# Moving the stores, the loads and the order of the units in an attention + gated-MLP kernel

## The chip, the cores and the metric

The kernel runs on one core of one Trainium2 chip. The time is device time in microseconds (us) of one execution. Executions of the same kernel spread by 1 to 3% within one call here, so every comparison of a few us is made with several runs, and the ratios quoted are the mean time of one kernel's fast runs over that of the other's of the same rounds; they are not quite the ratio of the medians that stand beside them. A run counts as slow when it is over 1.5% above the fastest run of the same kernel, or one die's clock is low; only fast runs enter a ratio.

Engines: PE is TensorE (matmuls), PEld its weight loads, DVE is VectorE, ACT is ScalarE, POOL is GpSimd, SP is SyncE, which here only issues DMAs. In these traces an instruction that waits holds what stands behind it in its engine's queue; the store on ACT below, behind which ACT stood idle for 2.30 us ahead of its next exponential, is an example.

## The reference, cut to what matters

```python
# q, k, v: [8 batches, 8 heads, 576, 64], float32
scores = q @ k.T / 8;  mask: 0 <= i - j < 64         # a sliding window of 64 keys
x = softmax(scores) @ v                               # -> [8, 576, 512]
h = relu(x @ w_in);  u, v = h[..., :512], h[..., 512:]
v_n = layer_norm(v)                                   # over the 512
v_s = w_spatial @ v_n + b_spatial                     # over the 576 positions
out = (u * v_s) @ w_out                               # float32
```

## The kernel before

For each batch, two chains of units run interleaved: the MLP of batch *a* and the attention of batch *a+1*. A string gives the order in which the units are put into the engines' queues; there is no other schedule.

| unit | PE does | ACT, DVE, POOL do |
|---|---|---|
| T*s* (batches 0 to 3) | transposes k and q of head pair *s* | copies of the result ("tr", turned k and q) |
| R*s* or T*s* (batches 4 to 7) | nothing | DVE turns k and q in 32 by 32 blocks |
| A*s* | scores of pair *s* ("sc"), product of pair *s−1* ("oz") | ACT exp, DVE mask; ACT ln, exp(−) ("ln", "zi"), DVE multiply to give "x" |
| F | – | the pending normalisation (zi, x), at once |
| V*j* | `x @ w_in[:, 512:]` for 128 positions ("pv") | ACT relu ("vs"), DVE statistics ("st", "mv") |
| Q | V of the last 64 positions, and the last 64 outputs of batch *a−1* | the same, and a store |
| L | – | layer norm: ACT ln, exp; DVE five "vn" |
| U*m*, G*m*, O*j* | `w_in[:, :512]` ("pu"), spatial ("ps"), `w_out` ("po") | ACT relu; DVE u·v_s ("g"); ACT copy to "ob", store |

"p0003" is V of batch 0 for the first 128 positions, summed over head pairs 0 to 2 (from 0 up to, not including, 3); "p0034" adds pair 3 and "o0" is the relu and the statistics that follow; W is the transposition of the spatial weights. Casts of k, q and v to 16 bits ("nk", "nq", "vn") and the shifted copy of v ("vs<-vn") run on POOL. "X4 of batch b" below means the last x (the remainder of 64 positions) of batch b.

The parts that the change touches:

```python
def load_pairs(b):                     # batches 0 to 3
    ...
    for s in range(4):
        for x in "kq": load_four(b, x, s)
        load_v_pair(b, s, nc.sync)
        if s == 2:
            for x in "kq": load_rest(b, x)     # the last 64 positions of k and q
    load_v_rem(b, nc.sync)

def T_out(b, s):                       # PSUM -> SBUF, y = 0 for k, 1 for q
    ...   (act_copy if b == 0 and y == 1 else dve_copy)(o[:, y, s, 0:512], tp[y][:, :])

def store(b, j, ob, p0):
    (nc.scalar if b < 3 else nc.sync).dma_start(out[b, ...], ob[...])
# ob = mpool.tile([128, 512], f32, tag="ob", bufs=3, ...)

for a in range(1, B):
    if a == 1: batch_in(2)                         # POOL casts of batch 2
    if a + 2 < B: load (a + 2)                     # at the start of the stage
    if a + 2 < B and a > 1: batch_in(a + 2)
    if a == 1:   run(a, "p0034 o0 p0134 o1 p0234 o2 p0334 o3 Q L U0 T0 U1 T1 A0 U2 ..."); batch_in(3)
    elif a == 2: run(a, "V0 T0 V1 T1 A0 V2 V3 Q T2 A1 L U0 U1 U2 T3 A2 ...")
    elif a == 3: run(a, "V0 V1 V2 V3 Q L T0 U0 U1 T1 A0 U2 ...")
    else:        run(a, "V0 V1 A0 V2 V3 Q A1 L U0 U1 U2 A2 U3 U4 G0 A3 ... R0 O0 O1 A5 O2 R1 O3")
```

The softmax here doesn't subtract the row's maximum and nothing guards it: scores larger than these inputs give would overflow.

## Time and profile before

260.36 us, median of three runs (258.87 to 261.31). I read the profile by stages. A stage goes from X4 of one batch to X4 of the next; it holds the MLP of that batch and the attention of the next. The table of windows of the kernel before, cut at those moments (columns: stretch in us, its length, busy time of each engine with the number of its instructions, the granted TensorE clock as a share of full speed, the busy share of the DMA engines, GB/s):

```profile
core 0: us, PE busy (x) PEld busy (x) DVE busy (x) ACT busy (x) POOL busy (x), PEclk, DMA share, GB/s
0.00:72.05 72.05, 56.59 (x575) 30.98 (x576) 40.80 (x90) 32.22 (x53) 47.80 (x81) 0.86 1.09 241
72.05:105.54 33.49, 27.02 (x314) 15.57 (x313) 21.48 (x41) 18.22 (x32) 20.73 (x30) 0.95 0.68 126
105.54:132.59 27.05, 26.05 (x315) 14.72 (x314) 20.04 (x40) 18.23 (x33) 6.90 (x9) 1.00 0.59 139
132.59:164.00 31.41, 25.91 (x357) 13.69 (x355) 21.56 (x38) 18.99 (x36) 13.39 (x14) 0.89 0.34 86
164.00:189.44 25.44, 23.50 (x352) 12.65 (x351) 17.50 (x33) 17.59 (x34) 12.97 (x14) 0.93 0.88 177
189.44:215.76 26.32, 24.37 (x356) 12.84 (x355) 18.30 (x36) 18.19 (x35) 13.02 (x15) 0.94 0.89 181
215.76:239.66 23.90, 22.78 (x356) 12.22 (x355) 16.11 (x33) 18.19 (x35) 0.17 (x1) 1.00 0.15 52
239.66:260.80 21.14, 17.30 (x114) 7.91 (x112) 9.03 (x21) 9.42 (x19) 0.00 (x0) 0.98 0.26 88
```

The first row is the start-up with batch 0 and the attention of batch 1; then one row for each of the batches 1 to 7. The stage without any loads or casts, 215.76 to 239.66, is the measure of the rest: 23.90 us, of which PE works 22.78. The stages of batch 1 (33.49) and of batch 3 (31.41) have little more busy time of PE (27.02 and 25.91) and take much more time; the start-up row holds more work, but PE is idle in 15.5 of its 72.05 us.

The granted clock over the whole span, in 40 slices of 6.5 us, in tenths (page of the kernel before):

```profile
PEclk9996897997598999999997799988999799999999
```

Each digit below 9 is a slice in which PE ran at half clock for a part. Matmuls of 512 columns take 0.63 us there instead of 0.38.

Part of the chain of waits of the kernel before in the hole after batch 0 (start, length, what):

```profile
52.84 6.26 DMA vf<-in_v_dram
...
59.12 0.02 ACTq L478
...
59.17 5.06 DMA out_dram<-ob
...
64.63 0.34 ACTq L478
...
65.01 0.64 ACT zi L423
```

And ACT's own timeline at the same place (start, length, engine, line, operation, in brackets the idle time before it):

```profile
53.45 0.58 ACT L568 COPY ob<-po 128x512 f32<-128x512 f32 x1
55.84 0.39 ACTq L478 DMA_DIRECT2D out_dram<-ob  x1
56.33 1.02 ACT L361 ACTIVATE e<-sc 128x1024 f16<-128x1024 f32 x1 [2.30 <-PE po L565]
```

Waits of PE for x over 162 to 240 us, and for the turned k and q in the stage of batch 3 (us in total, times, longest):

```profile
PE oz L396 <- DVE x L431: 5.0, 3, 2.0
```

```profile
PE sc L319 <- DVE tr L147: 3.8, 1, 3.8
```

The profiled execution took 262.51 us and counts as slow.

### The profile page before, as it was taken

The numbers are of one execution on the slowest core, as the hardware profiler recorded it, in microseconds if no ns is written. First come the engines' busy times: TensorE is split into PE (matmuls) and PEld (weight loads), VectorE is DVE, ScalarE is ACT, GpSimd is POOL, SyncE is SP. The second block draws the span as 40 slices with busy tenths as digits, with TensorE's granted clock in tenths as the row PEclk, the third lists the DMA queues.
The fourth block names the chain that finished last, engine by engine and source line by source line (L and its number), as shares of the span: only waits on it lengthen the run. The fifth ranks groups of instructions, "written<-read, shape, count | busy, mean of one in ns | idle before, by whom it ended". The sixth has DMA issues, their size and how long they took to land.

```text
span 260.8 us, 6702 instructions
## 1 busy us (share of the span) xinstructions
PE 223.5 (86%) x2725; PEld 120.6 (46%) x2725; DVE 164.8 (63%) x326; ACT 151.1 (58%) x271; POOL 115.0 (44%) x161
## 2 busy tenths in 40 slices
PE   8767889983885987999994998979997999899994
PEld 2533336651343653555542554535553555454441
DVE  5465185865268592797657387865796469563840
ACT  1454363255453564587574566875687568957713
POOL 3899258997026559920002980126913591000000
PEclk9996897997598999999997799988999799999999
DMA  6999999999997903877086003899499932004105
GB/s 196 247 250 226 203 244 224 246 241 325 247 180 179 147 3 100 219 149 161 32 239 117 3 3 123 193 201 171 126 227 199 183 114 92 23 4 156 27 0 181
DMA packets 77647, 40.43 MB, mean 155 GB/s; under 512 B 44272, under 2 KB 73008, under 8 KB 77616
## 3 DMA queue, kind: packets, MB, share of 16 engines
q1 hardware_dynamic: 73424, 34.22, 60.1%
q0 software_dynamic: 2224, 2.24, 5.1%
q10 hardware_dynamic: 1968, 3.54, 4.2%
q8 instruction: 21, 0.34, 0.6%
q14 instruction: 10, 0.08, 0.1%
HBM read 32.79 MB, written 9.44 MB: 162 GB/s over the span
## 4 chain that ended last, share of the span: by engine, by line
PE 47%; SPq 17%; DVE 16%; ACT 9%; DMA 7%; issue 3%; ACTq 1%
PE ps L546 11%; PE pv L459 7%; PE po L565 7%; SPq L122 7%; SPq L83 7%; PE pu L526 6%; DMA vf<-in_v_dram 5%; DVE vn L516 5%; DVE st L468 4%; PE oz L396 3%; PE sc L319 3%; SPq L87 3%; DVE x L431 2%; PE oz L406 2%; ACT e L361 2%
## 5 line engine op out<-in xcount | busy, mean ns | idle before, releaser
L361 ACT ACTIVATE e<-sc 128x1024 f16<-128x1024 f32 x32 | 32.8, 1024 | 35.7 <-PE sc L303 21.5
L177 POOL CAST nk<-fk 128x512 f16<-128x512 f32 (+2 forms) x23 | 18.8, 816 | 75.1 <-DVE tr L147 29.2
L431 DVE TENSOR_TENSOR x<-oz,zi 128x512 f16<-128x512 f32 (+1 forms) x40 | 25.3, 634 | 38.6 <-ACT zi L423 38.4
L177 POOL COPY vs<-vn 64x512 f16<-64x512 f16 (+1 forms) x56 | 44.5, 794 | 3.1
L377 DVE TENSOR_TENSOR e<-e,mask 128x1024 f16<-128x1024 f16 x32 | 27.8, 868 | 21.3 <-ACT e L361 21.0
L546 PE MATMUL ps<-wspT,vn 128*128 128x512 f16 (+1 forms) x160 | 39.3, 394 | 0.0
L459 PE MATMUL pv<-win,x 128*128 128x512 f16 (+1 forms) x132 | 34.3, 406 | 0.4 <-ACT vs L466 0.4
L526 PE MATMUL pu<-x,win 128*128 128x512 f16 x128 | 34.3, 418 | 0.0
L565 PE MATMUL po<-wout,g 128*128 128x512 f16 x128 | 31.1, 385 | 0.0
L177 POOL CAST vn<-vf 128x512 f16<-128x512 f32 (+1 forms) x40 | 26.9, 682 | 9.1 <-DMA vf<-in_v_dram 8.3
L468 DVE BATCH_NORM_STATS2 st<-vs 128x6 f32<-128x512 f16 (+1 forms) x40 | 26.9, 673 | 5.3 <-ACT vs L466 4.8
L414 ACT ACTIVATE ln<-oz 128x512 f32<-128x512 f32 (+1 forms) x40 | 22.2, 554 | 12.7 <-PE oz L406 12.3
L466 ACT ACTIVATE vs<-pv 128x512 f16<-128x512 f32 (+1 forms) x40 | 22.7, 596 | 9.0 <-PE pv L459 5.8
L177 POOL CAST nq<-fq 128x512 f16<-128x512 f32 (+2 forms) x27 | 21.3, 790 | 12.8 <-DMA fq<-in_q_dram 10.9
L423 ACT ACTIVATE zi<-ln 128x512 f32<-128x512 f32 (+1 forms) x40 | 23.4, 586 | 4.4 <-ACT ob L568 1.3
L549 DVE TENSOR_TENSOR g<-ps,ru 128x512 f16<-128x512 f32 x32 | 21.8, 686 | 6.6 <-PE ps L546 6.5
L568 ACT COPY ob<-po 128x512 f32<-128x512 f32 x32 | 18.6, 583 | 12.1 <-PE po L565 11.6
L396 PE MATMUL oz<-e,onesK 128*64 128x512 f16 x64 | 13.6, 417 | 13.1 <-DVE x L431 13.1
L546 PEld LDWEIGHTS <-vn 128*128 128x128 f16 (+1 forms) x160 | 15.2, 102 | 16.7 <-issue 1.9
L528 ACT ACTIVATE ru<-pu 128x512 f32<-128x512 f32 x32 | 17.2, 593 | 6.0 <-PE pu L526 6.0
L459 PEld LDWEIGHTS <-x 128*128 128x128 f16 (+1 forms) x132 | 12.8, 104 | 16.1 <-issue 3.2
L526 PEld LDWEIGHTS <-win 128*128 128x128 f16 x128 | 12.2, 105 | 16.0 <-issue 5.5
(97 smaller groups left out, 315.5 us busy)
## 6 DMA issues: line engine op xcount, KB each, us to landing
vf<-in_v_dram SPq DMA_DIRECT2D x40, 128.0 KB, 5.3
out_dram<-ob SPq DMA_DIRECT2D x20, 256.0 KB, 2.0
fk<-in_k_dram SPq DMA_DIRECT2D x32, 144.0 KB, 3.6
fq<-in_q_dram SPq DMA_DIRECT2D x32, 144.0 KB, 4.3
fk<-in_k_dram SPq DMA_DIRECT2D x16, 256.0 KB, 5.2
fq<-in_q_dram SPq DMA_DIRECT2D x16, 256.0 KB, 5.2
vf<-in_v_dram SPq DMA_DIRECT2D x16, 256.0 KB, 5.0
out_dram<-ob ACTq DMA_DIRECT2D x12, 256.0 KB, 3.1
```

The costliest lines, as they stand in the source:

```text
L177: nc.gpsimd.tensor_copy(o, i)
L361: nc.scalar.activation(e2[:, :, :], sc[0][:, :, :], AF.Exp, bias=0.0, scale=0.125)
L377: nc.vector.tensor_tensor(e2[:, :, :], e2[:, :, :], m, ALU.min)
L414: nc.scalar.activation(lnz[:, 0:n], OZ[b, s][:, 1, 0:n], AF.Ln)
L423: nc.scalar.activation(zinv[:, 0:n], lnz[:, 0:n], AF.Exp, bias=0.0, scale=-1.0)
L431: nc.vector.tensor_tensor(x[:, 0:n], oz[:, 0, 0:n], zinv[:, 0:n], ALU.mult)
L459: nc.tensor.matmul(PV[b, j][0:jn, :], xcol(b, r, j), w_in_sb[:, r, 512:1024], start=(r == 0), stop=(r == 3))
L466: nc.scalar.activation(vs[0:jn, :], pv[0:jn, :], AF.Relu)
L468: nc.vector.bn_stats(st6[0:jn, 0:6], vs[0:jn, :])
L526: nc.tensor.matmul(pu[:, :], w_in_sb[:, r, 128 * m:128 * m + 128], X[b, r][:, :], start=(r == 0), stop=(r == 3))
L546: nc.tensor.matmul(ps[:, :], VN[b, kk][0:kn, 128 * m:128 * m + 128], wspT[kk][0:kn, 0:512], start=(kk == 0), stop=(kk == 4))
L565: nc.tensor.matmul(po[:, :], G[b, r][:, 128 * j:128 * j + 128], w_out_sb[:, r, :], start=(r == 0), stop=(r == 3))
```

## The change

In a few words: all stores on the sync queue with five output buffers instead of three; the loads of the next but one batch behind the store in Q; V of batches 0 and 1 summed in two halves, two head pairs each, as the data lands; the turned k and q of the next batch, and the pending normalisation, ahead of layer norm; the copies of turned q on ACT. The diff, cut to its core ("..." and "cut" mark what is left out):

```diff
@@ load_pairs, batch_in: the remainder of k and q after pair 3's k and q, not before
-            load_v_pair(b, s, nc.sync)
-            if s == 2:
+            if s == 3:
                 for x in "kq":
                     load_rest(b, x)
+            load_v_pair(b, s, nc.sync)
@@ T_out: turned q always copied by ACT
-                (act_copy if b == 0 and y == 1 else dve_copy)(o[:, y, s, 0:512], tp[y][:, :])
+                (act_copy if y == 1 else dve_copy)(o[:, y, s, 0:512], tp[y][:, :])
@@ store
-        (nc.scalar if b < 3 else nc.sync).dma_start(out[b, ...], ob[...])
+        nc.sync.dma_start(out[b, ...], ob[...])
-        ob = mpool.tile([128, 512], f32, tag="ob", bufs=3, ...)      # twice
+        ob = mpool.tile([128, 512], f32, tag="ob", bufs=5, ...)
@@ run: loads and casts of batch a+2 in Q, after the store of batch a-1
                 if c == "Q":
                     emit_VO4(a)
+                    if a > 0 and a + 2 < B:
+                        load_any(a + 2)
+                        batch_in(a + 2)
@@ start-up and batch 0 (pairs 0, 1, 2, 3 with the remainder last; more warm-up matmuls; cut)
-    emit_S(0, 4)
-    E_exp(0, 4)
     ...
-    run(0, "p0003 p0103")            # V of batch 0: three of four pairs ...
+    run(0, "p0002 p0102")            # ... or two and two
     emit_P(0, 3)
+    emit_S(0, 4)
+    E_exp(0, 4)
     ...
-    emit_P(0, 4)
-    emit_N1(0, 4)
-    emit_N2(0, 4)
-    run(0, "p0034 o0 p0134 o1 p0234 o2 p0334 o3 Q L U0 U1 U2 U3")
-    run(0, "W0 W1 W2 W3 W4 U4 T0 G0 G1 T1 A0 G2 G3 T2 A1 G4 O0 T3 A2 O1 O2 T4 A3 O3")
-    run(0, "F A4 p1003 p1103 F A5 p1203 p1303 F")
+    emit_P(0, 4)
+    run(0, "p0023 p0123 p0223 p0323 p0034 o0 p0134 o1 p0234 o2 p0334 o3")
+    emit_N1(0, 4)
+    emit_N2(0, 4)
+    run(0, "U0 U1 Q L U2 T0 U3 A0 W0 W1 W2 W3 W4 U4 G0 T1 A1 G1 G2 T2 G3 A2 G4")
+    batch_in(2)
+    run(0, "O0 O1 T3 A3 O2 O3 T4 F A4 F p1002 p1102")
+    run(0, "A5 p1202 p1302 p1023 p1123 p1223 p1323 F")
@@ stages of batches 1 to 7
-  1: "... o3 Q L U0 T0 U1 T1 A0 U2 U3 T2 A1 ... G3 G4 A4 ..."
+  1: "... o3 T0 U0 T1 U1 A0 Q L T2 U2 U3 A1 ... G3 A4 G4 ..."
-  2: "... Q T2 A1 L U0 ..."                +  2: "... Q T2 A1 F L U0 ..."
-  3: "V0 V1 V2 V3 Q L T0 U0 U1 T1 A0 ..."  +  3: "V0 T0 V1 V2 V3 A0 Q F L T1 U0 U1 A1 ..."
-  4 to 7: "... Q A1 L U0 ..."              +  4 to 7: "... Q A1 F L U0 ..."
```

More of the change, by code (lines that the diff above doesn't have):

```diff
@@ L477, in store @@
         jn = 128 if j < 4 else 64
-        (nc.scalar if b < 3 else nc.sync).dma_start(out[b, 128 * j:128 * j + jn, :],
+        nc.sync.dma_start(out[b, 128 * j:128 * j + jn, :],
                                                     ob[p0:p0 + jn, :])
@@ L498, in emit_VO4 @@
             V_out(b, 4)
-        ob = mpool.tile([128, 512], f32, tag="ob", bufs=3, name=f"ob{o}_4")
+        ob = mpool.tile([128, 512], f32, tag="ob", bufs=5, name=f"ob{o}_4")
         nc.scalar.copy(ob[64:128, :], pv[64:128, :])
@@ L566, in emit_O @@
                                  start=(r == 0), stop=(r == 3))
-        ob = mpool.tile([128, 512], f32, tag="ob", bufs=3, name=f"ob{b}_{j}")
+        ob = mpool.tile([128, 512], f32, tag="ob", bufs=5, name=f"ob{b}_{j}")
         nc.scalar.copy(ob[:, :], po[:, :])
@@ L634, in run, with load_any @@
                     state["post"].pop(0)()
+    def load_any(b):
+        if b < NPE:
+            load_pairs(b)
+        else:
+            new_qkv(b)
+            load_batch(b)
     def v_in(b, s):
@@ L647, in batch_in @@
                 pairs_in(b, s, pool_copy, pool_copy)
+                if s == 3:
+                    pairs_in(b, 4, pool_copy, pool_copy)
                 v_in(b, s)
-                if s == 2:
-                    pairs_in(b, 4, pool_copy, pool_copy)
             v_in(b, 4)
@@ L659, in batch_in @@
                 shift_part(b, c // 2, pool_copy)
-    for s in (0, 1, 2, 4, 3):
-        pairs_in(0, s, dve_copy, pool_copy if s != 3 else dve_copy)
-        if s == 4:
-            emit_T(0, 4)
-            continue
+    for s in range(4):
+        pairs_in(0, s, dve_copy, pool_copy if s < 3 else dve_copy)
+        if s == 3:
+            pairs_in(0, 4, pool_copy, pool_copy)
         v_in(0, s)
@@ L670 @@
         T_mm(0, s)
+        if s < 3:
+            warm(2)
         if s > 0:
@@ L677 @@
         E_exp(0, s)
+        if s == 3:
+            T_mm(0, 4)
         if s > 0:
@@ L681 @@
             N_exp(0, s - 1)
-        warm(4)
+        if s < 3:
+            warm(4)
+    T_out(0, 4)
+    E_mask(0, 3)
+    N_mul(0, 2)
     v_in(0, 4)
@@ L687 @@
     batch_in(1)
+    run(0, "p0002 p0102")
+    emit_P(0, 3)
     emit_S(0, 4)
     E_exp(0, 4)
-    E_mask(0, 3)
-    N_mul(0, 2)
-    run(0, "p0003 p0103")
-    emit_P(0, 3)
     emit_N1(0, 3)
@@ L697 @@
     E_mask(0, 4)
-    run(0, "p0203 p0303")
+    run(0, "p0202 p0302")
     emit_P(0, 4)
+    run(0, "p0023 p0123 p0223 p0323 p0034 o0 p0134 o1 p0234 o2 p0334 o3")
     emit_N1(0, 4)
     emit_N2(0, 4)
-    run(0, "p0034 o0 p0134 o1 p0234 o2 p0334 o3 Q L U0 U1 U2 U3")
-    run(0, "W0 W1 W2 W3 W4 U4 T0 G0 G1 T1 A0 G2 G3 T2 A1 G4 O0 T3 A2 O1 O2 T4 A3 O3")
-    run(0, "F A4 p1003 p1103 F A5 p1203 p1303 F")
+    run(0, "U0 U1 Q L U2 T0 U3 A0 W0 W1 W2 W3 W4 U4 G0 T1 A1 G1 G2 T2 G3 A2 G4")
+    batch_in(2)
+    run(0, "O0 O1 T3 A3 O2 O3 T4 F A4 F p1002 p1102")
+    run(0, "A5 p1202 p1302 p1023 p1123 p1223 p1323 F")
     for a in range(1, B):
         if a == 1:
-            batch_in(2)
-        if a + 2 < B:
-            if a + 2 < NPE:
-                load_pairs(a + 2)
-            else:
-                new_qkv(a + 2)
-                load_batch(a + 2)
-        if a + 2 < B and a > 1:
-            batch_in(a + 2)
-        if a == 1:
-            run(a, "p0034 o0 p0134 o1 p0234 o2 p0334 o3 Q L U0 T0 U1 T1 A0 U2 U3 T2 A1 U4 G0 T3 A2 "
-                   "G1 G2 T4 A3 G3 G4 A4 O0 O1 A5 O2 O3")
-            batch_in(3)
+            run(a, "p0034 o0 p0134 o1 p0234 o2 p0334 o3 T0 U0 T1 U1 A0 Q L T2 U2 U3 A1 U4 G0 T3 A2 "
+                   "G1 G2 T4 A3 G3 A4 G4 O0 O1 A5 O2 O3")
         elif a == 2:
-            run(a, "V0 T0 V1 T1 A0 V2 V3 Q T2 A1 L U0 U1 U2 T3 A2 U3 U4 G0 T4 A3 G1 G2 G3 A4 "
+            run(a, "V0 T0 V1 T1 A0 V2 V3 Q T2 A1 F L U0 U1 U2 T3 A2 U3 U4 G0 T4 A3 G1 G2 G3 A4 "
                    "G4 O0 O1 A5 O2 O3")
         elif a == 3:
-            run(a, "V0 V1 V2 V3 Q L T0 U0 U1 T1 A0 U2 U3 A1 U4 G0 G1 A2 G2 G3 A3 G4 O0 A4 R0 O1 O2 "
-                   "A5 R1 O3")
+            run(a, "V0 T0 V1 V2 V3 A0 Q F L T1 U0 U1 A1 U2 U3 U4 A2 G0 G1 A3 G2 G3 A4 G4 R0 O0 O1 "
+                   "A5 O2 R1 O3")
         else:
-            run(a, "V0 V1 A0 V2 V3 Q A1 L U0 U1 U2 A2 U3 U4 G0 A3 G1 G2 G3 A4 G4 R0 O0 O1 A5 O2 R1 O3")
+            run(a, "V0 V1 A0 V2 V3 Q A1 F L U0 U1 U2 A2 U3 U4 G0 A3 G1 G2 G3 A4 G4 R0 O0 O1 A5 O2 R1 O3")
     run(B, "Q")
```

## The prediction

> What bounds the kernel now. One core, eight batches, read as stages (table of windows): start-up 0–33 us; batch 0 with attention of 1, 33–59; a hole 59–67; then 38, 27, 31.6, 26.3, 26.3, 23.8, 21.8 us. The late stages are bound by TensorE: 24.4 of 26.3 us busy at clock 0.94; in the 23.8 us stage (215–239, no loads or casts left) 22.7 at clock 1.00. The others lose time to waits:
> - 59–67: TensorE is busy 3.2 of 8 us, clock 0.68. The chain of waits runs through a store on the ACT queue (5.06 us to landing, behind loads) that holds one of three output buffers; then ACT zi, DVE x, PE oz.
> - 70–84: five layer-norm statistics in series (0.65 + 0.18 us each), five normalisations, 2.73 us together because GpSimd copies meanwhile (0.41 us each undisturbed), and only then the turned k and q (81.0) that the next scores wait for (2.3 us).
> - 137–142: TensorE busy 1.2 of 5 us; the turns of batch 4 stand behind layer norm (wait for DVE tr: 3.8 us).
> - Late: PE oz waits for DVE x, 5.0 us in three waits over 162–240, as x stands behind layer norm; the clock dips after (0.83 in 200–210).
> - Start-up: the remainder of k and q stands before pair 3; batch 0's last projections come after everything.
>
> Each hole also costs clock: the Trainium skill, "TensorE: Matmul & The Clock Gate", section "What's actually happening", says an idle window of about 3.4 us halves the clock. The trace agrees in kind: 512-column matmuls took 0.63 us instead of 0.38 after holes. The slow normalisations match "SBUF — State Buffer", "Who interferes with whom": VectorE and GpSimd exclude one another (1.24 against 0.41 us).
>
> What the change does. Work is the same, but for six warm matmuls (0.26 us each, in waits) and 12 copies of turned q moved from DVE to ACT (0.67 to about 0.6 us). The rest is order:
> - Start-up: pair 3 without the remainder ahead, half of V early: −3.5 us. Weights still bound it: issued at 14.5, 9.8 us to landing.
> - Stores on the sync queue, five buffers, batch 3's loads later: the hole mostly closes, −6 us.
> - Batch 1: turns ahead of layer norm: −6 us.
> - Batch 3: turns spread: −4 us.
> - Normalisation ahead of layer norm: −1 us in each of four stages, clock included.
> - Given back: loads of batches 5 to 7 start at the store in Q, some 6 us later in their stage. Those of k and q took 17 us to the last cast (163.7–180.7), V another 7.5. V would be ready some 7 us into the next stage, where the first attention product wants it at about 6. I add 3 us.
>
> Sum: −20.5. I take 241 us, a little less gain; range 233 to 252. Faster by over 2%: 0.94; within 2%: 0.05; slower: 0.01.
>
> Right if: no output copy on ACT waits for a store; batch 2's first V matmul comes at 88 to 92 us instead of 104; PE waits for DVE tr in batch 3's stage fall below 1 us; PE oz waits for DVE x below 2 us late; the clock holds 1.00 in more slices; TensorE's total busy time falls.
>
> Wrong if: the later loads make VectorE wait for GpSimd's casts in the last turn, or PE for V, in the stages of batches 4 to 6; stores behind loads in the one sync queue still fill five buffers; extra ACT copies delay exp; or the start-up waits for weights, so that reordering it gains nothing.

## The result, and the profile after

The changed kernel took 242.45 us (median of four runs, 241.97 to 245.32) beside 260.84 us for the kernel before (four runs). The ratio of the fast runs is 0.935, with a 95% interval of 0.927 to 0.944. The output is correct. The profiled execution (245.32 us) is the slowest of its four; keep that in mind for single stages.

The same table of windows of the changed kernel, again cut at X4 of each batch:

```profile
0.00:70.01 70.01, 54.04 (x578) 30.14 (x579) 35.98 (x85) 34.66 (x57) 47.95 (x82) 0.88 0.95 200
70.01:96.07 26.06, 24.48 (x309) 14.27 (x308) 17.88 (x37) 20.05 (x36) 11.97 (x19) 1.00 0.68 157
96.07:121.73 25.66, 25.66 (x316) 14.61 (x315) 18.40 (x36) 20.05 (x37) 7.04 (x10) 1.00 0.76 149
121.73:147.11 25.38, 23.19 (x356) 12.69 (x355) 19.54 (x38) 18.45 (x35) 14.75 (x18) 1.00 0.98 203
147.11:170.23 23.12, 22.89 (x356) 12.16 (x355) 17.80 (x35) 18.09 (x35) 10.98 (x12) 1.00 0.95 190
170.23:199.41 29.18, 25.89 (x356) 12.90 (x355) 19.67 (x35) 18.75 (x35) 18.60 (x22) 0.88 0.95 201
199.41:222.53 23.12, 22.76 (x356) 12.21 (x355) 16.11 (x32) 18.17 (x35) 2.85 (x4) 1.00 0.15 53
222.53:243.60 21.07, 17.30 (x114) 7.90 (x112) 9.02 (x20) 9.43 (x19) 0.00 (x0) 0.99 0.26 88
```

| stage | before | after | difference |
|---|---|---|---|
| up to X4 of batch 1 | 72.05 | 70.01 | −2.0 |
| batch 1 | 33.49 | 26.06 | −7.4 |
| batch 2 | 27.05 | 25.66 | −1.4 |
| batch 3 | 31.41 | 25.38 | −6.0 |
| batch 4 | 25.44 | 23.12 | −2.3 |
| batch 5 | 26.32 | 29.18 | **+2.9** |
| batch 6 | 23.90 | 23.12 | −0.8 |
| batch 7 and the end | 21.14 | 21.07 | −0.1 |

Two rows don't fit the total: the start-up gained almost nothing although the hole in it was to close, and the stage of batch 5 lost 6 us against its neighbours (29.18 against 23.12). The granted clock of the changed kernel in 40 slices of 6.1 us:

```profile
PEclk9997599599999999999999999999968999999999
```

Low clock is left in three places: slices 4 and 5, in the start-up, slice 8, in batch 0, and slices 30 and 31, in the stage of batch 5. Read from the records of the clock in the traces, PE had half clock for:

```
before (us):  20.9-27.7  41.4-44.8  61.9-72.1  82.4-85.8  140.4-147.2  174.5-177.9  201.8-205.2   sum 37.6
after  (us):  21.3-31.5  41.8-48.6  178.3-185.1                                                   sum 23.9
```

(the last fall, at the very end, left out). PE's busy time fell from 223.5 to 216.2 us, for the same matmuls and two warm-up matmuls more. Half of the 13.7 us less of half clock is 6.9 us, which is most of it.

Waits of PE of the changed kernel for the turned k and q in the stage of batch 3 (121 to 147 us), and its waits in the late stages (145 to 225 us):

```profile
PE sc L319 <- DVE tr L147: 1.3, 2, 0.9
```

```profile
PE oz L406 <- POOL vs L177: 3.5, 3, 2.1
PE oz L396 <- DVE x L431: 0.4, 1, 0.4
```

The waits for turned k and q and for x, on which the prediction built, are small now. A new one has come: PE waits for POOL's shifted copies of v. And in the start-up (timeline of PE of the changed kernel, and then of the kernel before, at the transposes of the spatial weights, L576):

```profile
22.23 1.89 PE L459 MATMUL pv<-win,x 128*128 128x512 f16 x4 [2.23 <-DMA win<-in_moe_w_in_dram]
...
42.50 0.64 PE L303 MATMUL sc<-tr 64*64 64x128 f16 x16 [3.05 <-DVE tr L180]
43.08 3.64 PE L576 MATMUL wps<-id,wnat 128*128 128x128 f16 x25
```

```profile
38.20 1.98 PE L576 MATMUL wps<-id,wnat 128*128 128x128 f16 x20 [0.58 <-ACT ru L528]
40.74 0.53 PE L576 MATMUL wps<-id,wnat 128*64 128x128 f16 x5 [0.57 <-DVE wspT L180]
```

In the changed kernel PE first stood 2.2 us for the weights `w_in`, then 3.05 us for a turned k that DVE delivers after layer norm, and the transposes behind it took 3.64 us at half clock instead of 2.5.

### The profile page after: what moved, and what is told of

Same layout as the page of the kernel before. It is cut to its first block, busy times and chain, and to the rows that moved or that the text cites. A ratio compares the mean times of both kernels' runs of the same rounds, so it can differ in the third digit from the quotient of the medians.

```text
span 243.6 us, 6712 instructions
## 1 busy us (share of the span) xinstructions
PE 216.2 (89%) x2727; PEld 116.9 (48%) x2727; DVE 154.4 (63%) x313; ACT 157.7 (65%) x283; POOL 114.1 (47%) x162
## 4 chain that ended last, share of the span: by engine, by line
PE 41%; DMA 20%; POOL 11%; ACT 9%; DVE 6%; SPq 6%; issue 5%; POOLq 0%; ACTq 0%
DMA fq<-in_q_dram 15%; PE ps L546 8%; PE pv L459 8%; PE po L565 7%; POOL vs L177 6%; PE pu L526 5%; SPq L117 4%; POOL vn L177 4%; DMA win<-in_moe_w_in_dram 3%; PE oz L396 2%; DMA vf<-in_v_dram 2%; ACT e L361 2%; DVE x L431 2%; PE oz L406 2%; DVE st L468 2%
## 5 line engine op out<-in xcount | busy, mean ns | idle before, releaser
L431 DVE TENSOR_TENSOR x<-oz,zi 128x512 f16<-128x512 f32 (+1 forms) x40 | 25.4, 635 | 29.2 <-ACT zi L423 29.1
L177 POOL CAST nk<-fk 128x512 f16<-128x512 f32 (+2 forms) x24 | 19.8, 825 | 48.2 <-DMA fk<-in_k_dram 39.8
L361 ACT ACTIVATE e<-sc 128x1024 f16<-128x1024 f32 x32 | 32.9, 1027 | 14.4 <-PE sc L303 10.1
L377 DVE TENSOR_TENSOR e<-e,mask 128x1024 f16<-128x1024 f16 x32 | 24.7, 772 | 21.6 <-ACT e L361 21.6
L546 PE MATMUL ps<-wspT,vn 128*128 128x512 f16 (+1 forms) x160 | 38.1, 384 | 0.0
L526 PE MATMUL pu<-x,win 128*128 128x512 f16 x128 | 33.2, 404 | 0.0
L466 ACT ACTIVATE vs<-pv 128x512 f16<-128x512 f32 (+1 forms) x40 | 23.2, 597 | 14.2 <-PE pv L459 12.3
L177 POOL CAST nq<-fq 128x512 f16<-128x512 f32 (+2 forms) x27 | 20.9, 776 | 23.8 <-DMA fq<-in_q_dram 23.7
L177 POOL CAST vn<-vf 128x512 f16<-128x512 f32 (+1 forms) x40 | 25.5, 642 | 12.4 <-DMA vf<-in_v_dram 11.5
L565 PE MATMUL po<-wout,g 128*128 128x512 f16 x128 | 30.1, 379 | 0.0
L423 ACT ACTIVATE zi<-ln 128x512 f32<-128x512 f32 (+1 forms) x40 | 23.7, 593 | 0.9
L546 PEld LDWEIGHTS <-vn 128*128 128x128 f16 (+1 forms) x160 | 14.6, 99 | 15.8 <-issue 0.7
L528 ACT ACTIVATE ru<-pu 128x512 f32<-128x512 f32 x32 | 17.9, 600 | 2.9 <-PE pu L526 2.5
L516 DVE TENSOR_SCALAR vn<-vs,mv,rs 128x512 f16<-128x512 f16 (+1 forms) x40 | 16.6, 482 | 2.4 <-ACT rs L508 2.4
```

Of the source, the lines that this page charges most:

```text
L177: nc.gpsimd.tensor_copy(o, i)
L361: nc.scalar.activation(e2[:, :, :], sc[0][:, :, :], AF.Exp, bias=0.0, scale=0.125)
L377: nc.vector.tensor_tensor(e2[:, :, :], e2[:, :, :], m, ALU.min)
L423: nc.scalar.activation(zinv[:, 0:n], lnz[:, 0:n], AF.Exp, bias=0.0, scale=-1.0)
L431: nc.vector.tensor_tensor(x[:, 0:n], oz[:, 0, 0:n], zinv[:, 0:n], ALU.mult)
L466: nc.scalar.activation(vs[0:jn, :], pv[0:jn, :], AF.Relu)
```

## The experiments

Twelve kernels ran and one more did not build. All twelve gave correct results. "Stage of batch b" is X4 to X4 as above; "X4(1)" is the time at which X4 of batch 1 is done. Medians of different calls come from different chips, so small differences are read from ratios and stages.

| kernel | median, us | ratio to before (fast runs) | X4(1) | stages of batches 1 / 2 / 3 / 4 / 5 / 6 |
|---|---|---|---|---|
| before | 260.36 | 1 | 72.1 | 33.5 / 27.1 / 31.4 / 25.4 / 26.3 / 23.9 |
| changed | 242.45 | 0.935 (0.927 to 0.944) | 70.0 | 26.1 / 25.7 / 25.4 / 23.1 / 29.2 / 23.1 |
| before + stores | 249.54 | 0.967 (0.961 to 0.973) | 64.3 | 32.9 / 26.5 / 30.6 / 23.0 / 24.2 / 23.9 |
| before + five buffers | 262.08 | 1.012 (1.000 to 1.024) | 72.4 | 33.6 / 27.1 / 31.4 / 25.5 / 26.3 / 23.9 |
| before + turns first | 252.33 | 0.980 (0.964 to 0.996) | 71.9 | 30.5 / 27.0 / 25.3 / 24.7 / 26.4 / 23.9 |
| before + norm first | 253.76 | 0.984 (0.974 to 0.994) | 72.6 | 33.9 / 26.7 / 30.3 / 22.3 / 23.1 / 23.1 |
| changed, q copies on DVE | 245.43 | 0.951 (0.945 to 0.956) | 72.6 | 27.1 / 26.1 / 24.7 / 23.9 / 24.3 / 23.9 |
| changed, loads early | 240.61 | 0.929 (0.922 to 0.936) | 69.7 | 26.1 / 25.7 / 25.2 / 23.1 / 23.1 / 23.1 |
| changed, old start-up | 238.31 | none (three of four runs slow) | 65.8 | 26.0 / 25.8 / 26.7 / 23.1 / 28.6 / 23.1 |
| changed, remainder first | 242.16 | 0.932 (0.919 to 0.945) | 69.1 | 26.4 / 25.7 / 24.8 / 23.7 / 24.7 / 23.5 |
| changed, W ahead of A0 | 239.39 | 0.926 (0.915 to 0.937) | 64.6 | 26.1 / 25.7 / 26.5 / 23.1 / 26.5 / 23.1 |
| changed, both mended, loads early | 236.21 | 0.905 (0.889 to 0.920) | 67.8 | 26.4 / 25.7 / 27.6 / 23.1 / 23.1 / 23.1 |
| **old start-up and loads early** | **233.75** | **0.907 (0.900 to 0.915)** | 64.4 | 25.6 / 25.7 / 25.7 / 23.1 / 23.1 / 23.1 |
| the same, all loads early | 235.04 | 0.905 (0.899 to 0.910) | 65.8 | 26.6 / 25.7 / 25.1 / 23.1 / 23.1 / 23.1 |

### 1. The stores, alone: queue or buffers?

Edit on the kernel before:

```diff
-        (nc.scalar if b < 3 else nc.sync).dma_start(...)
+        nc.sync.dma_start(...)
-  tag="ob", bufs=3      +  tag="ob", bufs=5
```

> The kernel before with one part of the change: all stores on the sync queue and five output buffers. Theory 1 (the hole at 59 to 67 us is the output buffer waiting for a store on the ACT queue): no wait for the store there, X of batch 1 complete at about 67 instead of 72.0, total 260.8 minus 5, about 256. Rival (the hole is the latency of the chain scores, exp, product, normalise at the end of batch 1 and needs no store): X of batch 1 still completes at 71 or later and the total falls by less than 1.5 us.

Measured: 249.54 us, ratio 0.967; by the ratio a gain of some 8.5 us where 5 were expected. X4(1) moved from 72.05 to 64.33. The stores are by themselves the largest single part of the gain. The stages of batches 4 and 5 are shorter too, but the kernel before had a dip of the clock there and this one none; in experiment 3 such dips are gone with another order of x and layer norm alone, and here they are gone without it, so I do not count that to the stores.

The prediction's mechanism was the lack of a free buffer. So, five buffers and nothing else:

```diff
-  tag="ob", bufs=3      +  tag="ob", bufs=5        # stores of batches 0 to 2 stay on ACT's queue
```

> The kernel before with five output buffers in place of three and nothing else: stores of batches 0 to 2 stay on the ACT queue. Theory 1 (the hole at 59 to 67 us is the lack of a free buffer): X of batch 1 complete at 64 to 66 us as with the stores on the sync queue, total about 250. Rival (it is the queue: ACT stands at its own stores, whatever the buffers): X of batch 1 at 70 us or later, total 258 or more.

Measured: 262.08 us, ratio 1.012, X4(1) at 72.35. The theory fell, the rival held: with the stores on ACT's queue five buffers change nothing. The trace of the kernel before agrees: none of its copies to "ob" waited for a buffer (the one at 63.21 us needed the buffer of a store that had landed at 61.10). The sync queue with three buffers was not run, so that the queue alone brings the whole gain is not shown. With the stores on sync the buffers are in fact used: in the changed kernel the copy at 169.73 us starts 6.1 us before the store three ahead of it has landed (175.88), so three buffers would have held ACT there. Waits of ACT over 50 to 68 us with five buffers and stores on ACT, then with five buffers and stores on sync (50 to 66 us):

```profile
ACT e L361 <- DMA fk<-in_k_dram: 5.4, 1, 5.4
ACT zi L423 <- DMA vf<-in_v_dram: 1.5, 1, 1.5
```

```profile
ACT e L361 <- PE sc L303: 3.1, 2, 2.5
ACT ln L414 <- PE oz L406: 2.2, 2, 1.2
```

In the first, an exponential on ACT stood 5.4 us for the landing of a *load of k*. ACT needs no k. The records of the trace show what lies between: the 200 DMAs of the SP and ACT queues count their landing on eight semaphores (numbers 101 and 103 to 109, 25 DMAs each), which loads and stores of both queues use one after the other, and none of the 200 issues starts before the earlier DMA on its semaphore has landed. In the kernel before:

```
store at 55.84 on ACT: waits for semaphore 106, last used by the load of k issued at 50.60, let go at 55.77
store at 59.17 on ACT: waits for semaphore 101, last used by the load of v issued at 52.84, let go at 59.10
store at 61.17 on ACT: waits for semaphore 106, last used by the store issued at 55.84,    let go at 61.10
store at 64.63 on ACT: waits for semaphore 101, last used by the store issued at 59.17,    let go at 64.23
```

From the end of ACT's last work to each of these stores ACT stood 1.8, 0.9, 0.5 and 0.8 us; with five buffers 4.9, 1.1, 0.0 and 0.3. These waits have moved to SP, where nothing stands behind them but other DMAs. The Trainium skill, "DMA: Bandwidth & Descriptors", section "Anatomy of one DMA — SWDGE (gpsimd) path", says in an aside that DMA engines do not wait on semaphores and that any such wait happens on the issuing sequencer before dispatch; this agrees. That 5.06 us store in the chain of waits, which I took for a held buffer, was a held semaphore. I could not take the semaphore alone away, so that sharing it is the cause rests on these records and on the two runs, not on a run of its own; it is argued, not shown.

### 2. The turns ahead of layer norm, alone

Edit on the kernel before: only the strings of batches 1 and 3, without F.

```diff
-  1: "... o3 Q L U0 T0 U1 T1 A0 U2 ..."      +  1: "... o3 T0 U0 T1 U1 A0 Q L T2 U2 ..."
-  3: "V0 V1 V2 V3 Q L T0 U0 U1 T1 A0 ..."    +  3: "V0 T0 V1 V2 V3 A0 Q L T1 U0 U1 A1 ..."
```

> The kernel before with one part of the change: in the stages of batches 1 and 3 the turned k and q of the next batch ahead of layer norm. Theory 1: stage of batch 1 (X of batch 1 to X of batch 2) from 33.5 to about 27.5 us, stage of batch 3 from 31.4 to about 27, the wait for DVE tr of 3.8 us gone, total about 10 us below the kernel before, 249. Rival (the stage of batch 1 was long for its late casts and its stores, that of batch 3 for its loads): each falls by less than 2 us.

Measured: 252.33 us where the theory had 249, ratio 0.980. The stage of batch 3 fell by 6.1 us to 25.3, and the wait for the turned k and q from 3.8 to 1.5 us: all of the changed kernel's gain in that stage. The stage of batch 1 fell by only 3.0 of the 7.4 us. The rest of it comes with other parts: 0.6 us with the stores alone, 1.1 us with the copies of q (experiment 4); 2.7 us come only when these meet and are not separated further.

### 3. The normalisation ahead of layer norm, alone

Edit on the kernel before: F in the strings of batches 2 and 4 to 7.

```diff
-  2: "... T2 A1 L U0 ..."      +  2: "... T2 A1 F L U0 ..."
-  4 to 7: "... Q A1 L U0 ..."  +  4 to 7: "... Q A1 F L U0 ..."
```

> The kernel before with one part of the change: the pending normalisation ahead of layer norm in the stages of batches 2 and 4 to 7. Theory 1 (x behind layer norm holds the next attention product and lets the clock fall): waits of PE for x in the late stages fall from 5.0 us to under 2, stages of batches 4 and 5 go from 26.3 to 24 or less, total 3 to 5 us below the kernel before. Rival (the dip of the clock there is chance; the run with only the stores changed had none without this part): late stages stay between 24 and 26, total within 2 us of the kernel before.

Measured: 253.76 us, ratio 0.984, some 4 us by the ratio. Waits of PE for x over 162 to 240 us of this run, to be set beside the 5.0 of the kernel before:

```profile
PE oz L396 <- DVE x L431: 1.0, 3, 0.4
```

The stage of batch 6, which had no dip before, gives the plain worth: 23.90 to 23.12 us. In the stages of batches 4 and 5 the dip of the clock is gone as well, and they fell by 3.2 us each; how much of that F brought is not shown, since the run with only the stores changed had no dip there either. The rival has a part of the truth: runs without F had these stages anywhere from 23.0 to 26.4 us. With F, and where v is not late, all of them lie at 23.1 within 0.1 us but for one at 22.3.

### 4. The copies of turned q on ACT, taken back

```diff
-                (act_copy if y == 1 else dve_copy)(...)
+                (act_copy if b == 0 and y == 1 else dve_copy)(...)
```

> The changed kernel with the twelve copies of turned q of batches 1 to 3 back on VectorE. Theory 1 (they matter little, since VectorE is 55 to 85% busy there): total within 1 us of the changed kernel, 242 to 243.5. Rival (they are an essential part of the gain of batches 1 and 2): stages of batches 0 to 2 grow by 1 us each, total 245 to 246.

Measured: 245.43 us, ratio 0.951 against 0.935, so my theory fell and the rival's total held. X4(1) came 2.6 us later and the stages of batches 1 and 2 grew by 1.1 and 0.4 us. A share of busy time (DVE 69%, ACT 77% in the stage of batch 1) did not show this: the copies stand between PE's transposes and its next scores. Up to X4(1), from 38 us on, PE's scores (L303) waited for turned k and q 5.7 us in all, against 4.3 in the changed kernel, and half clock was granted for 10.2 instead of 6.8 us. That two engines deliver k and q at the same time is how I read it; it has no run of its own.

### 5. The later loads

Edit on the changed kernel:

```diff
-                    if a > 0 and a + 2 < B:          # in Q
+                    if 0 < a < 3 and a + 2 < B:
 ...
     for a in range(1, B):
+        if 3 <= a and a + 2 < B:
+            load_any(a + 2)
+            batch_in(a + 2)
```

> The changed kernel, but for batches 3 to 5 the loads and casts of the next but one batch are issued at the start of the stage, as in the kernel before, instead of in Q after the store. Theory 1 (the later loads cost the stage of batch 5): the three waits of PE on GpSimd's vs copies in that stage (3.3 us) vanish, the stage from V of batch 5 to V of batch 6 goes from 29.2 us to 24 to 25, the whole from 242.5 to about 238. Rival (the transfers themselves are the limit, they take a whole stage whenever they start, or stores now queue behind loads and fill the five buffers): the stage stays above 27 us or others grow, and the total stays within 1 us of 242.5.

In the changed kernel, the stage of batch 5 at the place where PE needs batch 6's v (timeline of POOL and PE; the casts are named vn, the shifted copies vs):

```profile
172.50 0.62 POOL L177 CAST vn<-vf 128x512 f16<-128x512 f32 x1 [1.23 <-DMA vf<-in_v_dram]
...
175.86 1.17 POOL L177 CAST vn<-vf 128x512 f16<-128x512 f32 x2
...
177.09 2.48 POOL L177 COPY vs<-vn 64x1024 f16<-64x1024 f16 x2
...
178.18 0.22 PE L406 MATMUL oz<-e,vs 128*64 128x64 f16 x2 [2.08 <-POOL vs L177]
...
179.63 0.27 PE L406 MATMUL oz<-e,vs 128*64 128x64 f16 x2 [1.18 <-POOL vs L177]
...
179.88 0.13 PEld L526 LDWEIGHTS <-win 128*128 128x128 f16 x2
```

The loads of batch 6 were issued at 153.58 us, after the store in Q, where the kernel before had issued them at the start of its stage. So v was cast at 172.5 and 175.9, its last shifted copies end at 179.6, and the first product of batch 6 stood 2.08 and 1.18 us for them inside. The clock then fell (178.3 to 185.1), and twelve matmuls of U took 5.30 us. The wait of 3.3 us cost 6.1 us of stage.

With early loads, the same stage in the table of windows:

```profile
169.67:192.79 23.12, 22.76 (x356) 12.21 (x355) 18.67 (x36) 18.17 (x35) 13.83 (x16) 1.00 1.03 206
```

23.12 us, no such wait, clock 1.00. Over all runs the medians differ by less, 240.61 against 242.45 us, and the ratios by 0.6%, within their intervals: the changed kernel's profiled execution was its slowest, and it does not pay the whole price each time. In other runs with late loads the stage took 24.3 to 28.6 us. So the mechanism is shown; its worth is up to 6 us in a profiled execution, and some 2 us by the medians, which is not clear of the noise.

### 6. The new start-up against the old

Edit on the changed kernel: the order of loads, casts and units of the start-up and of batch 0 from the kernel before; stores, buffers, later loads and all other stages stay.

> The changed kernel with the start-up of the kernel before: remainder of k and q ahead of pair 3, V of batch 0 and of batch 1 not in halves, layer norm and U of batch 0 in the old order, casts of batch 2 issued at the start of batch 1's stage. Stores, five buffers, later loads and the rest stay changed. Theory 1 (the reordered start-up gained nothing, as it stands waiting for the weights at 20 to 22 us and lets the clock fall): X of batch 1 complete at 66 to 67 us instead of 70.0, the total 2 to 4 us below the changed kernel, about 239. Rival (the start-up order is what moved this point from 72.0 to 70.0): it goes back to 72 or more, and the total is 2 us or more above the changed kernel.

Measured: X4(1) at 65.75 us instead of 70.01, median 238.31 us. One run took 234.26 us, and the other three count as slow beside it, the profiled one too; experiment 7 has the same start-up in a fast profile with X4(1) at 64.39. The reordered start-up did not gain 3.5 us, it lost 4 to 6. Where? First suspect: the remainder's normalisation, which stands behind four relus and statistics.

```diff
     emit_P(0, 4)
-    run(0, "p0023 p0123 p0223 p0323 p0034 o0 p0134 o1 p0234 o2 p0334 o3")
     emit_N1(0, 4)
     emit_N2(0, 4)
+    run(0, "p0023 p0123 p0223 p0323 p0034 o0 p0134 o1 p0234 o2 p0334 o3")
```

> The changed kernel with two lines moved: the normalisation of batch 0's remainder tile comes ahead of the relu and the statistics of V, not behind them. Theory 1 (the new start-up loses because this normalisation stands behind four statistics on VectorE, so V of the remainder, layer norm and the next turned k come late): X of the remainder of batch 0 complete near 30 us instead of 35.6, layer norm done 2 us sooner, X of batch 1 at 67 to 68 instead of 70.0, total about 240.5. Rival (the new start-up loses in the wait for the weights, 2.2 us at half clock after it, whatever follows): X of batch 1 still at 69.5 or later.

Measured: X4 of batch 0 came at 31.7 instead of 35.6 us, but X4(1) only at 69.1, between the two expectations and nearer to the rival's; 242.16 us, ratio 0.932 against 0.935. The wait for the weights was 3.7 us in this run instead of 2.2; it differs from run to run. Counted from the first V matmul behind that wait, X4(1) came after 45.4 us instead of 47.8, so the remainder's place may be worth 2 us, and this one profile can't tell that from chance. Second suspect: the place of A0.

```diff
-    run(0, "U0 U1 Q L U2 T0 U3 A0 W0 W1 W2 W3 W4 U4 G0 T1 A1 ...")
+    run(0, "U0 U1 Q L U2 T0 U3 W0 W1 W2 W3 W4 U4 A0 G0 T1 A1 ...")
```

> The changed kernel with one unit moved in batch 0's sequence: the first scores of batch 1 (A0) behind the transposes of the spatial weights (W0 to W4) and U4, not ahead of them. Theory 1 (in the new start-up PE stands at these scores for 3.05 us until VectorE has done layer norm and the turned k, while W, U4 and warm work lie behind in its queue, and the clock halves, so W takes 3.6 us): the wait for the turned k falls below 1 us, W takes 2 to 2.5 us, X of batch 1 complete at 67 to 68 us instead of 70.0, total 239.5 to 241. Rival (the loss lies earlier, in the wait for the weights at 20 to 22 us, and anything later only absorbs it): X of batch 1 at 69.5 or later, total within 1 us of the changed kernel.

Measured: X4(1) at 64.56 us, 5.4 us sooner and more than I expected; 239.39 us. PE's timeline of this run at the same place as above:

```profile
37.60 1.49 PE L576 MATMUL wps<-id,wnat 128*128 128x128 f16 x15
39.32 0.52 PE L576 MATMUL wps<-id,wnat 128*128 128x128 f16 x5 [0.23 <-ACT wspT L183]
40.68 0.53 PE L576 MATMUL wps<-id,wnat 128*64 128x128 f16 x5 [0.85 <-DVE tr L180]
41.14 0.64 PE L532 MATMUL pu<-x,win 128*128 128x64 f16 x16
41.71 0.42 PE L303 MATMUL sc<-tr 64*64 64x128 f16 x16
```

The transposes need nothing from DVE's layer norm, so they fill the time in which PE had stood before A0; the scores (L303) start at 41.7 without a wait, and the five units behind no longer run at half clock. In the changed kernel, the end of batch 0's last G was at 58.60 us, here at 53.09; in the kernel before at 53.38. Not all of the 5.4 us belongs to the moved unit. The first transposes of batch 1 ("tp_0k"), which stand ahead of A0 in both strings, came at 35.74 instead of 37.55 us: half clock around the wait for the weights lasted 3.4 us in this execution and 10.2 in the changed kernel's, with the same program up to there. From those transposes to the end of the last G it is 17.35 us instead of 21.05. So the unit's place is 3.7 us of the loss, the largest part; the other 1.8 us lie at the weights, where half clock lasted longer.

> The changed kernel with the early loads for batches 5 to 7, and its own new start-up mended in two places: batch 0's remainder normalised ahead of the statistics, and A0 behind W and U4. If these two places are all that the new start-up loses against the old: X of batch 1 complete at 64 to 66 us and a total of 233 to 235, level with the version that has the old start-up. If the wait for the weights keeps its cost: X of batch 1 at 67 us or later, total 236 or more.

Both mends and the early loads together: 236.21 us, X4(1) at 67.8 in the profile, which was of a slow execution, so I compare its times only. Its two fast runs give the ratio 0.905, level with the best version, on a wide interval. PE waited 3.9 us for the weights there, 1.8 us more than with W ahead of A0 alone, and its first V matmul came 1.9 us later. Most of the rest of the 3.3 us lies between the first transposes of batch 1 and the last G (18.96 instead of 17.35 us), where half clock was granted for 3.4 us (43.8 to 47.2), and not at all with W ahead of A0 alone. So the expectation for a weight wait that keeps its cost (67 us or later) held for X4(1).

### 7. A version that beats both

Old start-up and early loads together on the changed kernel.

> The changed kernel with both of the parts taken back that cost time in their own runs: the old start-up, and the old place of the loads of batches 5 to 7. If the two effects are in different stages and simply add: X of batch 1 complete at about 65.8 us, stages of 26, 26, 26 and three of 23.1, last stage and end 21.1, total about 234 in the profile and 234 to 237 timed, below both the changed kernel and either of the two. If they interact (the earlier end of batch 1 meets loads that have not landed): one of the stages of batches 2 to 5 is 27 us or more, total 238 or more.

Measured: 233.75 us (six runs, 232.85 to 235.16), ratio 0.907 (0.900 to 0.915). The effects are in different stages and in the profiles they add: X4(1) came 5.6 us sooner than in the changed kernel and the stage of batch 5 is 6.1 us shorter, of 11.8 us in all. Table of windows of this run, the start-up and the stages of batches 1, 5 and 7:

```profile
0.00:64.39 64.39, 51.75 (x578) 29.33 (x579) 36.66 (x86) 34.04 (x57) 48.81 (x81) 0.95 0.99 217
64.39:90.01 25.62, 24.04 (x307) 14.07 (x306) 17.39 (x36) 20.05 (x36) 11.77 (x19) 1.00 0.63 164
...
164.52:187.63 23.11, 22.75 (x356) 12.20 (x355) 19.09 (x35) 18.16 (x35) 13.28 (x15) 1.00 1.05 209
...
210.76:231.80 21.04, 17.30 (x114) 7.91 (x112) 9.02 (x20) 9.42 (x19) 0.00 (x0) 0.96 0.26 88
```

Half clock was granted for 6.8 us in all before the end, against 37.6 us in the kernel before.

Then the loads of batches 3 and 4 at the start of their stages as well. The first build had the casts of batch 3 ahead of those of batch 2 on POOL and could not run (the build found a deadlock):

> The best version so far (old start-up, early loads of batches 5 to 7) with the loads of batches 3 and 4 at the start of their stages as well, so that no load waits for the store in Q any more. Theory 1 (putting loads behind the stores is worth nothing in any stage, the gain of the stores is their five buffers and not the distance to the loads): total within 1.5 us of 233.75, stages of batches 0 to 2 within 0.7 us. Rival (in the early stages loads and stores together slow one another and the distance matters, as the change intends): the stages of batches 0 and 1 grow by 2 us or more.

With the order mended:

```diff
-                    if 0 < a < 3 and a + 2 < B:          # in Q: now never
+                    if 0 < a < 1 and a + 2 < B:
-        if 3 <= a and a + 2 < B:
+        if 1 <= a and a + 2 < B:
+            if a == 1:
+                batch_in(2)
             load_any(a + 2)
             batch_in(a + 2)
```

> The best version so far (old start-up, early loads of batches 5 to 7; 233.75 us) with the loads of batches 3 and 4 at the start of their stages as well, so that no load waits for the store in Q any more (the first build of this had the casts of batch 3 ahead of those of batch 2 on GpSimd and could not run; the order is mended). Theory 1 (putting loads behind the stores is worth nothing in any stage; what the stores gain is that ACT no longer stands at them): total within 1.5 us of 233.75, the stages of batches 1 and 2 within 0.7 us of 25.6 and 25.7. Rival (in the early stages loads and stores together slow one another and the distance matters, as the change intends): the stages of batches 1 and 2 grow by 2 us or more.

Measured: 235.04 us, ratio 0.905 (0.899 to 0.910) against 0.907: the same. The stage of batch 1 took 26.6 instead of 25.6 us, a little more than the 0.7 us I allowed, that of batch 2 the same 25.7. Putting loads behind the stores, which the change names as its intent, is worth nothing that these runs can show in the early stages, and in the late ones it cost time in the profiled execution.

## Why the prediction was right or wrong

The total was right: 241 us predicted, 242.45 measured, within 233 to 252, and faster by more than 2%. Two of its six marks for being right were missed all the same (batch 2's first V matmul and the wait for DVE tr, below), and two of its conditions for being wrong came about: PE waited for V in the stage of batch 5, and the start-up waited for the weights while its new order gained nothing. Of its terms:

- **Start-up, −3.5 us: wrong, and of the wrong sign.** The step that failed is "pair 3 without the remainder ahead, half of V early: −3.5 us". V of batch 0 did start earlier (22.2 instead of 25.8 us; in other runs 22.8 to 24.9 with the old order and 21.3 to 24.2 with the new one), but the new string puts A0 ahead of W, and PE stood 3.05 us there and lost the clock. Against the old order with all else changed, the new start-up cost 4 to 6 us, of which A0's place is 3.7. I had costed what moved forward and not looked at what came to stand behind a wait in PE's queue. The warning that "the start-up waits for weights" was right: 2.2 us, and up to 10.2 us of half clock around it, which differs from run to run.
- **Stores, −6 us: near in size, wrong in mechanism.** The stores with the buffers moved X4(1) by 7.7 us. "Holds one of three output buffers" failed: five buffers alone moved it by nothing. What held ACT was the issue of the store itself, by the records on a semaphore that a load still held. That the size came out near is luck. In the changed kernel the two terms, −7.7 and +4 to 6, left −2.0, which is why batch 2's first V matmul came at 95.4 us and not at 88 to 92.
- **Batch 1, −6 us: right** (−7.4), but the turns alone gave 3.0 of it; the cost of 12 copies of q on ACT instead of DVE, which I took for neutral, was a gain of 1.1 us here and 2.6 us before.
- **Batch 3, −4 us: right, larger** (−6.0). The wait for DVE tr fell from 3.8 to 1.3 us, not below 1 as forecast.
- **Normalisation first, −1 us in each of four stages: right.** 0.8 us where no dip was; up to 3.2 us where the dip was gone too; 4 us alone, in all. PE waits for x late are 0.4 us.
- **Given back, +3 us: right.** It was named with its place (v late for the first product in the stages after batch 4), and it came in the stage of batch 5: +2.9 us against before, 6.1 us against the same stage with early loads in the profiled runs, some 2 us on average.
- PE's busy time fell and the clock is at full speed in 35 slices instead of 29: right.

So the total was right partly because two errors cancelled: a loss in the start-up that I had booked as a gain, and gains in the middle stages that were larger than booked. That part of it is luck.

## What to carry to other kernels

Put DMA issues on a queue where nothing else stands behind them: the price of a store on a computing engine is not its 0.34 us of issue but the wait in front of it, here up to 4.9 us (with five buffers) for a load that the engine had no interest in. In an in-order queue, ask of each unit that waits what independent work lies behind it, and put that work ahead; one unit's place was worth 3.7 us here. When a change has several parts, test them one by one even after it won: two of this one's parts cost time, and the version without them took 233.75 us instead of 242.45. When two profiles differ, cut the difference at a point that the edit can't have reached: part of what looked like the worth of A0's place lay ahead of it.

## What the Trainium skill lacked or had wrong

- "DMA: Bandwidth & Descriptors", section "Issuing engines are not separate DMA queues", says that issuing from several engines only saves the time to initiate a DMA, "which is usually small relative to the DMA itself". Here moving 15 stores from ACT's queue to the sync queue (with two buffers more, which did nothing while the stores stayed on ACT) took the kernel to 0.967 of its time; by the records the issuing engine waits ahead of the issue. The section does not name that wait.
- No page that I read says that DMAs of different queues may hold one another up over a shared landing semaphore. In this program a store on ACT waited for a load of k (issued at 50.60, let go at 55.77 us) that was issued by another engine; "DMA: Bandwidth & Descriptors" speaks of shared semaphores only as a risk of reading too early.
- "TensorE: Matmul & The Clock Gate", section "What's actually happening", gives the half clock "after ≥1 idle window (~3.4µs)". The window need not be idle throughout: in the changed kernel the clock fell at 178.28 us, when PE had been idle for 2.1 of the 3.41 us before, and in the kernel before at 41.39 us after only 0.8 us idle in such a stretch. (A later section of that page does tell of a kernel whose short idle times between groups of matmuls let the clock go up and down; the row by itself is too narrow.) The steps of about 3.4 us do agree: the low stretches ahead of the end last 3.4, 6.8 or 10.2 us, and 13.65 us in two runs.
- "SBUF — State Buffer", section "Who interferes with whom", which the prediction leans on, has nothing wrong here: layer norm's normalisations took 0.41 us alone and up to 1.24 us beside one of GpSimd's casts. The page limits the exclusion to VectorE instructions that use the port pair shared with GpSimd; the prediction's sentence is wider than that.
